# Bias products as units of their own, q and k in quarters, and a newly planned queue in a fused attention and maxout kernel

## The chip, the cores and the metric

The kernel runs on one core of one Trainium2 chip. The metric is the device time of one execution in microseconds (us), the median of several runs. The engines that matter here: PE (TensorE, matrix products), DVE (VectorE), ACT (ScalarE), POOL (GpSimd), and SP (SyncE), which issues nearly all DMAs. Each works through its own queue in program order; semaphores order them among each other.

## The reference

`q`, `k` and `v` have 4 batches, 8 heads, 768 tokens and a head size of 64. The attention is local and global: a token sees the 96 last tokens up to itself and the first 8 tokens of its sequence, with a bias that falls with distance. The result `x` (3072 tokens by 512) goes through a layer that takes the maximum of three products, and one more product.

```python
keep = is_global | is_local              # key position < 8, or 0 <= i - j < 96
scores = scale * q @ k.T - slopes[h] * dist
a = softmax(where(keep, scores, -1e9))
x = (a @ v), heads side by side          # 3072 x 512
h = maximum(maximum(x @ w1, x @ w2), x @ w3)   # 512 -> 768
out = h @ w_out                          # 768 -> 512, float32
```

## The kernel before, in words

The 3072 tokens are 24 tiles T of 128 (6 in each batch). Two tiles make a group G = 0 to 11, which is loaded together. Attention is done tile by tile, against the tile itself and the one before it. The 8 keys of the sequence's start are put into places of the key tile that the local window doesn't reach. The layer that follows is done in chunks c = 0 to 6 of 4, 2, 2, 4, 4, 4 and 4 tiles (`SIZES`), 512 or 256 columns wide, for 6 blocks f of 128 hidden units and 3 weight matrices j.

No scheduler orders the work. The string `SCHEDULE` lists some 770 units; each issues a few instructions, and an engine does what it is given in the order of the list. A unit's name is its code and its arguments, and after `@` the buffer slot that it fills. The waits between engines follow from which buffers the instructions read and write; so the list decides only who stands ahead of whom. The list is the output of a planner outside the kernel.

The units that the text speaks of (line numbers are those of the profile):

- `l` loads q, k (a = 0, 1) or v (a = 2) by DMA on SP (L220). Group number 12 stands for the first four tiles of q or k together, loaded as two halves of four heads (L213). `c` casts them to bf16 (L185), `v` casts v (L238). The last argument of a unit that can run on several engines says which: 0 ACT, 1 DVE, 2 POOL (POOL does a cast in two halves).
- `x` transposes q or k on PE (L252 for the first four tiles, L258 else), `y` copies the result from PSUM (L266, L269). `X` does the same by a DMA transpose.
- `K` and `B` make the tables of masks and biases (L350, L345), after `R`.
- `S T.g.how` makes the scores of a tile for four heads (L321). With `how` = 1 the bias is first put into the same bank by a product with the identity (L313); else `m` multiplies the exponential by a mask on DVE (L337, L339). `e` is the exponential on ACT (L328), from PSUM.
- `A` multiplies the weights with v (L363, L366), `n` divides by the sums on DVE (L374, L375). `t` and `u` transpose the tile on PE and copy it (L390, L393), or `Z` does so by a DMA transpose (L396).
- `G` and `V` put the global keys and values in place (L289 and L291, L299 and L301).
- `w`, `W` and `q`, `Q` load and cast the weights (L488, L185, L497).
- `F c.f.j` is a block of the first layer, 4 products (L405). `f c.f.j` drains it: j = 0 copies the bank (L419, ACT or DVE), j = 1 and 2 take the maximum on DVE (L421, L424).
- `O c.i` is the second layer of one tile, 6 products (L429), `o` copies it from PSUM (L444), `s` stores it (L450), in one DMA or several.
- `E` is the whole second layer of the last chunk, the last tile in pieces of 256, 128 and 128 columns with a copy and a DMA each (L434, L435).
- `D n.w` issues n products of zeros with w columns (L506), fillers on PE.

PSUM has 8 banks. F, O, x and t take one, a pair of scores or an A takes two. A unit that fills a bank waits until the last reader of its former content is through: F waits for an f, S or A for an e or n. The output staging of `o` and `E` uses the buffers of the loaded weights, `wst0` and `wst1`.

Before the first F, PE has the queue's transposes of the first four tiles and of group 2, the scores of tiles 0 to 5, and A and t of tiles 0 to 3, in both queues.

Of the kernel before, what the change touches and what calls it, by code (L numbers as in the profile page):

```python
# [12 lines left out]
FP32 = mybir.dt.float32  # L13
# [36 lines left out]
    V9.1.1 m10.0.1 S10.1.0@0 e10.1@6 V9.0.0 G10.1 O1.1@7 F2.5.1@2 f2.5.1.1 t8@3 F2.4.1@0 O0.0@1 m10.1.1 X11  # L50
    S11.1.0@4 l1.7.2@0 f2.4.0.0@4 o1.1.0@2 e11.1@4 v11.0.0 u8.1@0 S11.0.0@2 v10.0.1 f2.4.1.1 A10@6 V10.0.2
    e11.0@7 V10.1.0 X12@2 o0.0.1@2 n10@0 F2.5.2@0 F2.0.2@1 X13 l2.8.2@0 F2.1.0@4 F2.1.2@5 F2.1.1@2 F2.0.1@3
    m11.1.1 f2.5.2.1@0 Z9 F2.4.2@0 Z10 m11.0.1 f2.1.0.0@1 f2.1.1.1 l2.6.2@1 f2.4.2.1 A11@6 n11@3 O1.0@2
    o1.0.0@1 t11@0 u11.0 F2.3.2@4 l0.7.2@1 f2.1.2.1 f2.0.1.1 f2.0.2.1 f2.3.2.1 F2.2.2@3 l0.8.2@2 v12.0.2
    v12.1.2 v13.1.2 s1.1 f2.2.2.1 v13.0.2 S12.0.0@6 e12.0@1 c0.7.2.2@0 S13.0.0@0 l1.8.2@3 l1.9.2@4 S13.1.0@4
    v16.1.2 S12.1.0@2 l2.7.2@2 F3.0.0@6 G12.1 G13.2 e13.1@2 e13.0@0 e12.1@3 m12.1.1 F3.1.1@7 c1.7.2.2
    F3.0.1@4 m12.0.1 F3.5.0@5 m13.0.1 f3.5.0.1@4 F3.4.0@0 f3.4.0.0@1 f3.0.0.0@3 f3.0.1.1 F3.1.0@1 f3.1.0.0@2
    m13.1.1 F3.1.2@0 F3.5.1@1 v16.0.2 f3.1.1.1 v14.1.2 F3.3.0@6 A13@2 F3.3.2@7 c1.8.2.0@2 F3.5.2@4 V13.1.0
    c1.9.2.0@1 F3.2.1@5 f3.5.1.1 c0.8.2.1 n13@1 V13.0.1 F3.4.1@1 F3.2.0@2 f3.2.0.0@0 f3.1.2.1@1 f3.5.2.1
# [5 lines left out]
    S17.1.0@6 v19.0.0 V15.0.0 e17.1@1 e17.0@3 V15.1.0 O2.0@5 F4.4.0@6 m16.0.1 v19.1.0 s0.1 s3.2 s0.3 s1.0
    o3.0.0@0 m17.1.1 m17.0.1 f4.4.0.1@4 o3.3.1@1 m16.1.1 F4.2.0@7 o3.1.0@0 F4.2.1@0 F4.4.1@1 F4.4.2@4
    f4.4.1.1 F4.3.0@1 A16@2 V16.1.2 f4.2.0.0@0 o2.0.0@1 f4.2.1.1 f4.4.2.1@1 n16@1 X19@1 F4.3.1@0 X18
    S18.1.0@4 f4.3.0.0@2 f4.3.1.1 e18.1@5 S19.1.0@2 V16.0.2 v18.1.2 S19.0.0@6 e19.0@6 m19.0.1 S18.0.0@0
    F4.2.2@4 F4.1.2@5 e18.0@4 l2.10.2@0 m18.1.1 m18.0.1 e19.1@7 A17@0 m19.1.1 F4.5.0@6 f4.5.0.0@1 l1.10.2@6
# [516 lines left out]
```

## Time and profile before

| | |
|---|---|
| median of 3 runs | 176.38 us (176.31 to 176.66) |
| the profiled execution | 176.6 us |
| its span, first to last instruction | 174.7 us |
| PE busy, products | 166.9 us (96%) |
| DVE busy | 127.7 us (73%) |
| ACT busy | 102.4 us (59%) |
| POOL busy | 48.9 us (28%) |
| DMA, moved | 37.35 MB, 214 GB/s in the mean |

The page gives busy times of each engine and the costliest groups of instructions by line. The order of time lists instructions with start and duration, and in brackets how long the engine was idle before and what ended that. The busy time by stretches lists, for each, its length, then the busy time of PE, weight loads, DVE, ACT and POOL with counts, the granted clock, the busy share of the DMA engines and their GB/s. The chain that ended last follows the work back from the last instruction; its rows are start, length and what was run. A busy PE row ends at a modelled end, later than the moment at which the next product may start.

### The profile page before, as it was taken

The numbers are of one execution on the slowest core, as the hardware profiler recorded it, in microseconds if no ns is written. First come the engines' busy times: TensorE is split into PE (matmuls) and PEld (weight loads), VectorE is DVE, ScalarE is ACT, GpSimd is POOL, SyncE is SP. The second block draws the span as 40 slices with busy tenths as digits, with TensorE's granted clock in tenths as the row PEclk, the third lists the DMA queues.
The fourth block names the chain that finished last, engine by engine and source line by source line (L and its number), as shares of the span: only waits on it lengthen the run. The fifth ranks groups of instructions, "written<-read, shape, count | busy, mean of one in ns | idle before, by whom it ended". The sixth has DMA issues, their size and how long they took to land.

```text
span 174.7 us, 3862 instructions
## 1 busy us (share of the span) xinstructions
PE 166.9 (96%) x1489; PEld 93.5 (54%) x1510; DVE 127.7 (73%) x259; ACT 102.4 (59%) x153; POOL 48.9 (28%) x94
## 2 busy tenths in 40 slices
PE   7799999999999999999999999999999999999992
PEld 2346745576956867644456445554444554444442
DVE  7798969784868988589697287839859993059930
ACT  5979895487995876746257994721375651310022
POOL 4056536349370300196614003200203210000000
PEclk9999999999999999999999999999999999999999
DMA  5999999999999898998989498999992134047106
GB/s 148 352 292 312 363 351 379 294 319 345 270 230 267 193 145 194 290 319 198 232 146 196 119 253 200 290 159 260 272 184 68 32 90 64 0 180 240 60 10 234
DMA packets 66658, 37.35 MB, mean 214 GB/s; under 512 B 24144, under 2 KB 61904, under 8 KB 66640
## 3 DMA queue, kind: packets, MB, share of 16 engines
q1 hardware_dynamic: 66496, 37.04, 84.5%
q8 instruction: 12, 0.20, 0.5%
q10 hardware_dynamic: 144, 0.07, 0.1%
q14 instruction: 6, 0.05, 0.1%
HBM read 25.17 MB, written 6.29 MB: 180 GB/s over the span
## 4 chain that ended last, share of the span: by engine, by line
PE 83%; DVE 5%; DMA 4%; ACT 3%; issue 2%; SPq 1%; ACTq 0%
PE psum L405 50%; PE psum L429 18%; PE psum L321 5%; DMA rawqq<-in_q_dram 4%; PE psum L363 4%; PE psum L366 3%; PE psum L258 2%; DVE qkT L266 1%; ACT P L328 1%; PE psum L390 1%; DVE h L421 1%; DVE P L337 1%; PE psum L313 1%; SPq L213 1%; ACT qb L185 1%
## 5 line engine op out<-in xcount | busy, mean ns | idle before, releaser
L405 PE MATMUL psum<-xT,w 128*128 128x512 bf16 (+1 forms) x491 | 99.3, 348 | 1.1
L405 PEld LDWEIGHTS <-w 128*128 128x128 bf16 x504 | 47.5, 98 | 43.1 <-issue 2.7
L328 ACT ACTIVATE P<-psum 128x1024 bf16<-128x1024 f32 (+1 forms) x48 | 43.3, 953 | 13.5 <-PE psum L321 13.2
L421 DVE TENSOR_TENSOR h<-h,psum 128x512 bf16<-128x512 bf16 (+1 forms) x42 | 24.6, 604 | 16.1 <-PE psum L405 12.6
L429 PE MATMUL psum<-wo,ht 128*128 128x512 bf16 (+2 forms) x148 | 32.9, 362 | 0.6 <-issue 0.3
L337 DVE TENSOR_TENSOR P<-P,wmask 128x1024 bf16<-128x1024 bf16 x35 | 23.8, 695 | 6.2 <-ACT P L328 6.1
L424 DVE TENSOR_TENSOR ht<-h,psum 128x512 bf16<-128x512 bf16 (+1 forms) x42 | 26.1, 643 | 3.0 <-PE psum L405 2.4
L419 ACT CAST h<-psum 128x512 bf16<-128x512 f32 (+1 forms) x32 | 15.6, 517 | 20.1 <-PE psum L405 17.9
L429 PEld LDWEIGHTS <-ht 128*128 128x128 bf16 x156 | 14.0, 98 | 14.1
L238 POOL CAST va<-rawv 64x512 bf16<-64x512 f32 x26 | 16.5, 636 | 13.6 <-DMA rawv<-in_v_dram 12.8
L375 DVE TENSOR_TENSOR xb<-psum,rz 128x512 bf16<-128x512 f32 x24 | 16.6, 691 | 0.8
L299 POOL COPY va<-vaf 4x260 int32<-4x260 int32 x15 | 5.9, 395 | 37.5 <-PE psum L366 37.2
L321 PE MATMUL psum<-qkT 64*128 64x128 bf16 x352 | 14.9, 217 | 1.2 <-DVE qkT L266 0.9
L321 PEld LDWEIGHTS <-qkT 64*128 64x128 bf16 x352 | 10.3, 94 | 9.6 <-issue 6.8
L363 PEld LDWEIGHTS <-P 128*128 128x128 bf16 x192 | 12.3, 97 | 2.4
L363 PE MATMUL psum<-va,P 128*128 128x65 bf16 x160 | 12.5, 193 | 0.1
L444 ACT COPY ost<-psum 128x512 f32<-128x512 f32 x11 | 6.4, 589 | 8.9 <-PE psum L429 8.2
L366 PEld LDWEIGHTS <-P 128*128 128x128 bf16 x160 | 10.4, 97 | 1.5 <-issue 0.3
L434 ACT COPY ost<-psum 128x512 f32<-128x512 f32 (+2 forms) x5 | 2.3, 480 | 15.1 <-PE psum L429 15.0
L366 PE MATMUL psum<-va,P 128*128 128x65 bf16 x128 | 9.9, 193 | 0.0
L301 ACT COPY va<-vaf 4x520 bf16<-4x520 bf16 x10 | 6.2, 620 | 3.8 <-PE psum L366 3.7
L374 DVE RECIPROCAL rz<-psum 128x8 f32<-128x8 f32 x24 | 4.8, 202 | 4.7 <-PE psum L366 3.7
(69 smaller groups left out, 134.4 us busy)
## 6 DMA issues: line engine op xcount, KB each, us to landing
rawv<-in_v_dram SPq DMA_DIRECT2D x12, 512.0 KB, 6.3
rawq<-in_q_dram SPq DMA_DIRECT2D x10, 512.0 KB, 7.3
rawk<-in_k_dram SPq DMA_DIRECT2D x10, 512.0 KB, 7.0
out_dram<-ost SPq DMA_DIRECT2D x19, 256.0 KB, 2.6
wst<-in_moe_w_dram SPq DMA_DIRECT2D x3, 1024.0 KB, 10.9
wst<-in_moe_w_dram SPq DMA_DIRECT2D x3, 512.0 KB, 8.1
wost<-in_moe_w_out_dram SPq DMA_DIRECT2D x3, 512.0 KB, 7.3
out_dram<-ost SPq DMA_DIRECT2D x9, 128.0 KB, 1.8
```

What stands on the lines that cost most here:

```text
L238: copies[how](heads(va(T))[64 * e:64 * e + 64, :, 0:D], src)
L321: nc.tensor.matmul(sp[:, hh, j2, ds], qT(T - ds, 1)[hsl, jp], qT(T, 0)[hsl, jp], start=not how, stop=True, skip_group_check=True)
L328: nc.scalar.activation(P[:, :, 0:n], sps[T, g].rearrange("p a b d n -> p (a b) d n")[:, :, 0:n], AF.Exp, bias=0.0, scale=scale)
L337: mul(P, P, wmask[:, g, :, 0:2])
L363: nc.tensor.matmul(o, P[:, i, 0], heads(va(T))[:, h], start=True, stop=(t == 0), skip_group_check=True)
L366: nc.tensor.matmul(o, P[:, i, 1], heads(va(T - 1))[:, h], start=False, stop=True, skip_group_check=True)
L375: nc.vector.tensor_tensor(out=x.rearrange("p (g h) d -> p g h d", g=2), in0=o4[:, :, :, 0:64], in1=rz[:, :, :, None].to_broadcast([128, 2, ...
L405: nc.tensor.matmul(ps, w123[f // 2][:, j, dm, (f % 2) * 128:(f % 2) * 128 + 128], xT[c][:, dm], start=(dm == 0), stop=(dm == 3))
L419: copies[how](h01, ps)
L421: nc.vector.tensor_max(h01s[c, f], h01s[c, f], ps)
L424: nc.vector.tensor_max(dst, h01s[c, f].rearrange("p (t e i) -> p t e i", e=2, i=64), ps.rearrange("p (t e i) -> p t e i", e=2, i=64))
L429: nc.tensor.matmul(po, ht[c][:, f, tt * 128:(tt + 1) * 128], wo[:, f, cols], start=(f == 0), stop=(f == NF - 1))
```

## The change

- **Bias units.** The product that puts the bias into the bank leaves `S` and becomes the unit `b T.g`, which takes the bank's slot. `S` with `how` = 1 adds to it and carries no slot. Seven scores have a bias, as before.
- **Quarters.** The half of q and k that is loaded second (heads 0 to 3 of the first four tiles) is loaded, cast and transposed as two quarters of two heads. `span4` had these parts already; the list used none. A cast on POOL can now be cut along the second dimension too, and the buffer `qkT` of the first two groups is laid out so that each `y` writes one stretch.
- **Staging.** The stores get twelve slots `os` of their own size, laid over the memory of `wst1`, in place of slots of `wst0` and `wst1`.
- **The queue.** The whole list is planned anew, with each buffer held until the instruction that reads it has ended. Units move between engines: DVE takes 15 of the 42 first copies `f` (10 before), 6 of the 20 `o` (9), 2 of the 9 `W` (4), 11 `V` (7), 10 `v` (6); ACT takes 4 of the casts `c` of later groups (9) and 4 `V` (10); POOL 13 such casts (8). One of the two fillers `D3.256` goes. `O5.0` with its copy and its store, now in two DMAs, stands behind `E`.

The diff, cut to its core; of the list, the start, the places named in the text, and the end:

```diff
-    l0.12.1@0 l1.12.1@1 R K4 K3 K6 B4.1 B0.1 K5 K0 K2 B1.0 K7 B6.0 B2.1 l1.12.0@2 B3.1 c0.12.1.1@0 B7.1
-    l0.12.0@3 l2.0.2@0 l2.1.2@1 l0.2.2@4 c1.12.1.1@1 l1.2.2@5 w0.1@0 B5.1 D10.512@0 w0.0@1 x12.0.1@0
-    y0.0.1.0@0 w0.2@2 D3.256@1 x12.1.1@1 y0.1.1.1 S0.1.1@2 c1.12.0.1 c0.12.0.1 S1.1.0@4 K1 x12.1.0@6
-    y0.1.0.1 G0.2 y1.0.1.0@1 e1.1@0 m1.1.1 v0.0.2 v1.0.2 e0.1@1 v0.1.2 D3.256@0 x12.0.0@0 y0.0.0.0 S1.0.1@2
...
-    S6.1.0@4 F0.4.2@2 f0.4.2.1 e7.1@5 F1.5.0@3 F1.1.0@0 m7.1.1 e7.0@6 m7.0.1 F1.3.0@1 F1.5.1@2 x4.1.2@6
...
-    f6.0.1.1 f6.0.2.1 f6.3.2.1 s4.0.2 s4.3.2 s5.2.2 F6.5.0@0 f6.5.0.1@0 F6.5.1@3 f6.5.1.1 F6.5.2@1 f6.5.2.1 E@0
+    l0.12.1@0 l1.12.1@1 D10.512@0 l1.12.3@2 l0.12.2@3 l0.12.3@4 R K7 K6 B1.1 K4 B2.1 K2 B3.0 K1 K5 B0.1 B6.1
+    K0 c0.12.3.2@0 l1.12.2@5 c0.12.1.1 B4.1 B5.1 c1.12.1.1@1 K3 x12.0.1@0 y0.0.1.0@0 B7.1 l2.0.2@0 D3.256@1
+    x12.1.1@1 b0.1@2 v1.0.2 l2.1.2@1 c1.12.3.1 v1.1.2 b1.0@4 y0.1.1.0 b1.1@6 S1.1.1 l0.2.2@6 c0.12.2.1
+    y1.0.1.1@1 y1.1.1.0 x12.0.2@0 e1.1@0 c1.12.2.1 x12.0.3 y0.0.0.1 l1.2.2@0 y1.0.0.1 x12.1.3@1 x12.1.2
...
+    V1.1.1 V1.0.2 G2.1 v3.1.2 w0.2@2 A0@2 S3.0.1 e3.0@6 b3.1@6 n1@0 c0.2.2.2@2 S3.1.1 G3.0 A2@0 V2.0.2
+    e3.1@7 V2.1.2 n0@1 t0@2 W0.0.2 c1.2.2.1 u0.0@0 x2.1.2@3 y2.1.2.0@2 w1.2@2 x2.0.2@2 A3@4 t1@6 u1.0 n2@2
+    y2.0.2.1 t2@7 n3@3 l0.3.2@1 l1.3.2@2 S4.1.0@0 V3.1.2 e4.1@0 V3.0.2 S4.0.0@2 W1.1.2 u2.1 t3@6 G4.1 u3.0
+    W2.0.1 S5.1.0@4 e5.1@2 S5.0.0@0 e5.0@1 m4.1.1 W1.0.1 e4.0@3 F0.5.0@7 F0.4.0@6 W2.1.0 F0.3.0@4 f0.3.0.0@0
...
+    f1.0.1.1 f1.2.0.1@0 Q0.2 f1.0.2.1@1 x3.1.2@6 y3.1.2.1@3 F0.4.2@5 f0.4.2.1 l1.4.2@3 v6.0.2 Q1.2 F1.1.0@0
+    F1.2.2@1 l0.4.2@4 l1.6.2@5 F1.2.1@4 f1.2.1.1 F1.3.1@2 f1.2.2.1 F1.3.2@3 v7.0.2 F1.3.0@4 f1.3.0.0@2
+    f1.3.1.1 f1.3.2.1 x3.0.2@1 F0.5.2@5 f0.5.2.1 F1.4.0@2 F1.1.1@3 f1.1.0.0@3 y3.0.2.0 S6.0.0@0 S6.1.0@4
+    G6.2 c1.4.2.2@1 c0.4.2.2 l0.5.2@0 c0.5.2.2@2 f1.1.1.1 f1.4.0.0@1 e6.0@4 S7.0.0@6 S7.1.0@2 l1.5.2@6
+    c1.5.2.2 e6.1@5 c1.6.2.2@0 e7.1@6 F1.4.1@0 e7.0@7 l2.4.2@1 O0.2@1 f1.4.1.1 m7.1.1 x4.1.2@0 F1.5.2@2
...
+    m10.1.1 e11.0@0 f2.0.0.0@1 A10@2 V10.0.2 f2.1.1.1 m11.1.1 o1.0.0@4 n10@3 Z8@0 V10.1.0 l0.7.2@2 v11.1.2
+    v15.1.2 v12.1.2 F2.5.2@0 O1.1@1 v12.0.2 S12.1.0@2 e12.1@3 S13.1.0@4 m11.0.1 Z9 f2.5.2.1 S13.0.0@6
+    o1.1.1@5 F2.4.2@0 A11@2 n11@2 F2.0.1@1 e13.1@1 F2.3.1@4 m12.0.1 m12.1.1 e13.0@2 c0.7.2.1@1 Z10 f2.0.1.1
...
+    s4.1 f6.1.0.0@1 s3.0 s5.3.2 f6.3.1.1 f6.1.1.1 f6.3.2.1 f6.2.1.1 F6.2.2@2 f6.2.2.1 f6.1.2.1 F6.5.1@4
+    F6.5.0@1 f6.5.0.1@2 F6.5.2@5 f6.5.1.1 f6.5.2.1 E@7 O5.0@2 o5.0.0@5 s5.0.2
...
+    staging = persist.tile([128, 2048 * RINGS["wst1"] + 1024 * RINGS["wst0"]], FP32, name="staging")
+    staged = {"wst1": (0, 2048), "os": (0, 512), "wst0": (2048 * RINGS["wst1"], 1024)}
...
-        n = src.shape[1]
-        for lo, hi in (((0, n // 2), (n // 2, n)) if how == 2 else ((0, n),)):
-            copies[how](dst[:, lo:hi], src[:, lo:hi])
+        if how != 2:
+            copies[how](dst, src)
+            return
+        first = src.shape[1] > 1
+        n = src.shape[1 if first else 2] // 2
+        for half in (slice(0, n), slice(n, 2 * n)):
+            s = (slice(None), half) if first else (slice(None), slice(None), half)
+            copies[how](dst[s], src[s])
...
-            qkT[G] = ring("qkT", slot, [128, 2, 2, NP, 128], BF16, "qkT")
+            shape = [128, 2, 2, 2, NP // 2, 128] if G < 2 and QUAD_USED else [128, 2, 2, NP, 128]
+            qkT[G] = ring("qkT", slot, shape, BF16, "qkT")
...
+    def u_b(slot, T, g):
+        n = 2 if T % NT else 1
+        sp = ring("sp", slot, [128, 2, 2, 2, 128], FP32, "sp")
+        sps[T, g] = sp
+        for hh in range(2):
+            nc.tensor.matmul(sp[:, hh, :, 0:n], identb, bias[:, g, hh, :, 0:2] if n == 2 else bias[:, g, hh, :, 2:3],
+                             start=True, stop=False, skip_group_check=True)
...
     def u_S(slot, T, g, how):
-        if how:
-            for hh in range(2):
-                nc.tensor.matmul(sp[:, hh, :, 0:n], identb,
...
+        if not how:
+            sps[T, g] = ring("sp", slot, [128, 2, 2, 2, 128], FP32, "sp")
+        sp = sps[T, g]
...
-        osts[c, tt] = ring(("wst0", "wst1")[chunks[c][tt] % 2], slot, [128, DM], FP32, "ost")
+        osts[c, tt] = ring("os", slot, [128, DM], FP32, "ost")
```

More of the change, by code (lines that the diff above doesn't have):

```diff
@@ L50 @@
[L50 to L59, printed above, removed]
@@ L65 @@
[L65 to L69, printed above, removed]
@@ L93 @@
-LAST_STAGES = ((2, 1, 0), (2, 0, 1))
+RINGS = {'r': 7, 'rv': 3, 'qb': 3, 'qkT': 4, 'sp': 2, 'h': 8, 'P': 8, 'xb': 4, 'xT': 3, 'wst0': 3, 'wst1': 3, 'ht': 2, 'h01': 5, 'rz': 4, 'os': 12}
+LAST_BANKS = (6, 7, 3, 0, 1, 4, 5, 2)
+LAST_STAGES = (8, 2, 0, 10, 11, 7, 6, 3, 4, 9, 1, 5)
 @with_exitstack
@@ L157, in ring @@
         assert 0 <= slot < RINGS[name]
+        if name in staged:
+            first, width = staged[name]
+            first += slot * width
+            flat = staging[:, first:first + math.prod(shape[1:])]
+            return flat if len(shape) == 2 else flat.rearrange("p (i f) -> p i f", i=shape[1])
         return pools[name].tile(shape, dtype, name=label, tag=f"{name}{slot}")
```

126 lines of the change are left out of this document (66 added, 60 removed).

## The prediction

> **What bounds the kernel now.** I read first the page's totals, then the busy time by stretches, then the chain that ended last.
>
> ```profile
> span 174.7 us, 3862 instructions
> PE 166.9 (96%) x1489; PEld 93.5 (54%) x1510; DVE 127.7 (73%) x259; ACT 102.4 (59%) x153; POOL 48.9 (28%) x94
> PEclk9999999999999999999999999999999999999999
> ```
>
> TensorE is busy 96% of the span and its clock is granted throughout. The busy time by stretches shows where the rest lies:
>
> ```profile
> 24.00:40.00 16.00, 15.89 (x129) 9.44 (x130) 13.74 (x25) 10.49 (x17) 6.91 (x12) 1.00 1.12 331
> 40.00:60.00 20.00, 19.82 (x240) 14.69 (x241) 15.46 (x36) 16.47 (x27) 10.22 (x19) 1.00 1.06 257
> 60.00:80.00 20.00, 19.52 (x190) 12.30 (x193) 15.97 (x34) 13.09 (x21) 6.47 (x11) 1.00 1.03 245
> ...
> sum 144.00, PE 142.23 PEld 79.42 DVE 108.51 ACT 79.79 POOL 38.40; mean PE 20.32 PEld 11.35 DVE 15.50 ACT 11.40 POOL 5.49
> ```
>
> The first number after each stretch's length is PE's busy time. From 24 to 168 us PE is idle for 144.00 - 142.23 = 1.77 us in all. That is nearly everything that a better order can win in the middle (a little more hides behind matmul ends, which are modelled). The new queue has the same 126 F, 24 A, 48 S and 20 O units, and a score run still stands between products of another shape 15 times after the first F in both, so PE's own work there is unchanged. The kernel's time is therefore the **start** (until the first F, L405), the **middle** (PE's work plus its idle) and the **tail** (after PE's last product). The change is judged in these three.
>
> **The start: quarters and bias units.** The chain, the order of time and the groups by shape give the prices:
>
> ```profile
> 17.69 0.89 PE psum L258 x16
> ...
> 19.24 0.24 PE psum L390 x4
> ...
> 21.59 0.32 PE psum L405
> ```
>
> ```profile
> 9.23 1.72 SPq L220 DMA_DIRECT2D rawk<-in_k_dram  x1
> 9.39 0.69 DVE L185 CAST qbq<-rawqq 128x1024 bf16<-128x1024 f32 x1 [0.33 <-DMA rawqq<-in_q_dram]
> ...
> 9.58 0.49 PE L506 MATMUL psum<-zeros 128*128 128x256 bf16 x3
> ...
> 15.40 1.05 ACT L185 CAST qb<-rawq 128x1024 bf16<-128x1024 f32 x1
> ...
> 16.34 1.95 ACT L328 ACTIVATE P<-psum 128x1024 bf16<-128x1024 f32 x2
> ...
> 16.69 0.67 DVE L185 CAST qb<-rawk 128x1024 bf16<-128x1024 f32 x1
> ...
> 18.17 1.01 ACT L269 COPY qkT<-psum 128x1024 bf16<-128x1024 bf16 x1
> ...
> 18.62 0.69 DVE L269 COPY qkT<-psum 128x1024 bf16<-128x1024 bf16 x1
> ```
>
> For the k at 9.23 alone, the time from issue to landing:
>
> ```profile
> DMA to landing us min/median/max: 7.3/7.3/7.3
> ```
>
> ```profile
> L328 ACT ACTIVATE P<-psum 128x1024 bf16<-128x1024 f32 x40 | 39.3, 1022 | 11.9 <-PE psum L321 11.5
> ...
> L328 ACT ACTIVATE P<-psum 128x512 bf16<-128x512 f32 x8 | 4.8, 603 | 1.7 <-PE psum L321 1.7
> ...
> L393 ACT COPY xT<-psum 128x512 bf16<-128x512 bf16 x3 | 1.8, 587 | 1.5 <-PE psum L390 1.5
> ```
>
> ```profile
> L375 DVE TENSOR_TENSOR xb<-psum,rz 128x512 bf16<-128x512 f32 x24 | 16.6, 691 | 0.8
> ...
> L374 DVE RECIPROCAL rz<-psum 128x8 f32<-128x8 f32 x24 | 4.8, 202 | 4.7 <-PE psum L366 3.7 <-PE psum L363 0.7
> ```
>
> The last half of q is cast at 9.39 for 0.69 us now. In quarters the cast that stands last is half as long (about 0.35, an estimate from that row), and so is the block of transposes behind it: some 0.6 us is won there. The three bias units (b0.1, b1.0, b1.1) run before their scores' operands are ready, in PE time that is idle; later, each still costs what it cost inside S. One filler of 0.49 us (9.58) goes; it lay in idle time, so it is worth nothing. Two more issues on SP cost nothing, since SP issues far ahead of the landings there.
>
> But the gain does not reach the first F. k of group 2 (tiles 4 and 5) is issued at 9.23 and lands 7.3 us later, at 16.5, as its cast at 16.69 shows. The same bytes stand ahead of it in the new queue, so it lands at 16.5 again; its cast ends at 17.3 again. The new order then puts both transposes of group 2 (x2.1, x2.0) before A3. x2.0 takes bank 2, which u0.0 empties on ACT after e3.1. The two e3 ran 16.34 to 18.29; with the 1.05 us cast at 15.40 moved to POOL they end about 0.9 earlier, at 17.4. So u0.0 ends at 18.0 (0.59), x2.0 at 18.45 (half of the 0.89 row), A3 near 18.95 (at most the 0.66 that now lies between 18.58 and 19.24). On DVE y2.0.2.1 (0.69, as at 18.62) stands before n3: it starts 0.2 after x2.0, ends at 19.3, and n3 (0.20 + 0.69) at 20.2. t3 is done near 20.6. On ACT stand y2.1 (1.01, to 19.0), u1.0 (behind t1, 19.35 to 19.95), e4.1 (1.02, to 20.95) and then u3.0, to 21.55. The first F starts near 21.6, against 21.59 now: **0**. Bounds: -0.9, if what ACT wins passes through whole, and +0.7, one unit late on POOL, where a cast of 1.05 us on ACT becomes two of about 0.7.
>
> **The middle: the order planned anew.** Nothing computes less. By the groups, DVE takes five more first copies (f with j = 0) and five fewer copies of O and W between them; with the small ones its sum grows by about 2 us, ACT's falls by about 7 and POOL's grows by about 5. The held-buffer rule adds no instruction: the waits were always in the program, only the order is chosen differently.
>
> ```profile
> 41.84 0.24 PE psum L321 x4
> 42.07 0.02 issue
> 42.10 0.61 ACT P L328
> 42.70 0.04 issue
> 42.74 0.38 PE psum L405
> ```
>
> This is the kind of stall that such a rule should remove: the first S of a run writes a bank, its exponential (L328) must read it, and an F of the same bank stands too near. The chain runs through L328 here: it ends at 42.70 and the F starts at 42.74. It costs PE one or two tenths, since other S run meanwhile: all of PE's idle time from 40 to 60 us is 0.18. The old queue has this form three times (S6.0.0 to F0.4.2, S12.0.0 to F3.0.0, S18.1.0 to F4.2.2), the new one once (S6.0.0@0 to F1.4.1@0, with three S between and a half exponential of 0.60: about 0.05). But it has others, where DVE is late:
>
> ```profile
> L337 DVE TENSOR_TENSOR P<-P,wmask 128x1024 bf16<-128x1024 bf16 x35 | 23.8, 695 | 6.2 <-ACT P L328 6.1
> L424 DVE TENSOR_TENSOR ht<-h,psum 128x512 bf16<-128x512 bf16 x30 | 21.0, 724 | 2.6 <-PE psum L405 2.1
> L421 DVE TENSOR_TENSOR h<-h,psum 128x512 bf16<-128x512 bf16 x30 | 19.9, 681 | 15.0 <-PE psum L405 12.6 <-ACT h L419 2.0
> ...
> L424 DVE TENSOR_TENSOR ht<-h,psum 128x256 bf16<-128x256 bf16 x12 | 5.2, 440 | 0.4 <-PE psum L405 0.3
> ```
>
> F1.3.0@4 takes the bank of F1.2.1, whose maximum stands on DVE behind y3.1 (0.69) and f0.4.2 (0.72): about 0.5. S12.1.0@2 takes A10's bank, emptied by n10, which stands behind m11.1 (0.70): 0.2. F2.4.2@0 waits for f2.5.2 (0.44) behind m11.0 (0.70): 0.25. F0.0.1@1 waits for f0.5.1 (0.68): 0.15. With the 0.05 that is about 1.15 us in some 38 us. A part of each stall, the last matmul's modelled end, counts as PE busy, so perhaps 0.6 of it would show as idle. The old kernel shows 0.11 + 0.18 + 0.48 = 0.77 over the 56 us from 24 to 80. So I take the middle at **0**, with ends at -1.8 (all of PE's idle goes) and +1.8 (it doubles).
>
> **The tail: O5.0 after E.** In the old queue E is last, and E ends in small pieces:
>
> ```profile
> 171.63 0.27 ACT L434 COPY ost<-psum 128x128 f32<-128x128 f32 x1 [0.34 <-PE psum L429]
> 171.93 0.37 ACTq L435 DMA_DIRECT2D out_dram<-ost  x1
> ```
>
> ```profile
> L444 ACT COPY ost<-psum 128x512 f32<-128x512 f32 x11 | 6.4, 589 | 8.9 <-PE psum L429 8.2
> ```
>
> Outputs issued on SP in a row, and the time from issue to landing of all outputs after 156 us:
>
> ```profile
> 156.92 3.29 SPq L450 DMA_DIRECT2D out_dram<-ost  x7
> ```
>
> ```profile
> DMA to landing us min/median/max: 1.7/1.9/2.2
> ```
>
> In the new queue `O5.0@2 o5.0.0@5 s5.0.2` follow E. PE ends at the same time, since six products are only moved. But the last copy is 512 wide, 0.59 instead of 0.27: +0.32. Its output goes out in two DMAs on SP, one behind the other: seven issues in 3.29 us are 0.47 each, so the last is issued 0.47 after the first: +0.45 or so. The landing takes 1.7 to 2.2 either way. Nothing runs beside it, PE is done. Tail: **+0.75**; ends +0.3 (the second DMA's issue hides behind the first's landing) and +1.0.
>
> **The sum.** The profiled execution took 176.6 for its span of 174.7; the median of the runs is 176.38, so I take 0.2 off. 176.6 + 0 + 0 + 0.75 - 0.2 = 177.15, say **177.1**.
>
> **The rivals.** (1) *Faster: the bank stalls go.* The new order holds a bank until its reader ends, and the waits of the form at 42.10 go, with the other idle. To show, it must win the tail's 0.75 back and some 0.35 more, out of the 1.77 or at the start. For it: three such stalls become one. Against: the four DVE places. At 1.5 in the middle and 0.4 at the start: 176.4 + 0.75 - 1.9 = 175.2. (2) *No change:* the middle or the start wins just what the tail loses, or the tail's second DMA hides: 176.4. It is also the case in which the change does not do what it says, as the plan's rule has no instruction of its own. (3) *Slower still: DVE becomes the bound* around the change from chunk 0 to 1 and from 2 to 3, and the F behind it wait bank after bank: 177.1 + 1.5 = 178.6. For it: DVE's load grows there while PE's doesn't; against: its 73%. (4) *The PE clock falls* when the filler at 9.58 goes and PE pauses for loads. The products of some 2.5 us between 7 and 12 us would take twice as long, 177.1 + 2.5 = 179.6. The first fillers show the lower rate:
>
> ```profile
> 1.19 4.45 PE L506 MATMUL psum<-zeros 128*128 128x512 bf16 x10 [1.19 <-DVE cap L524]
> ```
>
> Ten of 512 columns in 4.45 us are about 0.44 each. The three of 256 in 0.49 (at 9.58) are at most 0.16 each, and their last end is a modelled one, so the rate by column had risen by then. The Trainium skill, "TensorE: Matmul & The Clock Gate", section "The HAM clock gate", says that the clock halves after an idle window of about 3.4 us. By that rule it would not fall here: the longest pause that I find in the new order is below 1 us. No run here shows such a fall.
>
> **How the numbers follow.** Forecast (177.1, 176.75 to 177.8) 0.42; rival 1: 0.22; rival 2: 0.15; rival 3: 0.18; rival 4: 0.03. About 0.2% (0.35 us) is what a measurement of this kernel can tell from no change. Faster 0.22, same 0.15, slower 0.42 + 0.18 + 0.03 = 0.63. The range reaches from 175.4, near rival 1, to 178.6, rival 3, and leaves out less than 0.2.
>
> **What would show it.** Start: the first L405 product at 21.6 (right) or before 21.0 (wrong). Middle: PE's idle from there to the last F near 1.8 us; below 0.7, rival 1; above 3 with DVE as releaser, rival 3. Tail: the last line in time is L450 on SP twice, 0.47 apart, after a 0.59 us copy, and the span ends 0.75 us later after PE's last product than now. If PE's last product comes over a microsecond earlier, the forecast is wrong.

## The result and the profile after

| | before | after |
|---|---|---|
| median | 176.56 us (176.21 to 177.12, 20 runs) | 176.09 us (175.03 to 177.06, 20 runs) |
| ratio, 95% interval | | 0.997 (0.9958 to 0.9982) |
| the profiled execution, its span | 176.6, 174.7 | 176.69, 174.8 |

The change makes the kernel 0.3% faster, about 0.5 us. The forecast was 177.1, slower. The profiled execution of after lies 0.6 us above its median; a second profile of the same kernel (e1 below, 176.16, span 174.4) lies at it, so both are used.

The totals of the page after, as those shown of before:

```profile
span 174.8 us, 3865 instructions
...
PE 165.9 (95%) x1485; PEld 93.6 (54%) x1507; DVE 131.9 (75%) x268; ACT 95.4 (55%) x147; POOL 54.7 (31%) x99
...
PEclk9999999999999999999999999999999999999998
```

DVE's sum grew by 4.2 us, ACT's fell by 7.0, POOL's grew by 5.8 (forecast: 2, 7 and 5). The clock is granted until the last slice, most of which lies behind PE's last product. The busy time by stretches of after (PE's is the first number behind the length):

```profile
24.00:40.00 16.00, 15.89 (x122) 9.07 (x123) 12.31 (x24) 11.17 (x16) 8.21 (x13) 1.00 1.05 345
40.00:60.00 20.00, 19.83 (x232) 14.85 (x233) 16.11 (x34) 14.00 (x23) 14.49 (x25) 1.00 1.06 235
60.00:80.00 20.00, 19.18 (x211) 12.40 (x212) 17.56 (x41) 11.92 (x19) 4.28 (x9) 1.00 1.10 246
80.00:100.00 20.00, 19.14 (x183) 9.88 (x186) 16.90 (x31) 11.04 (x15) 6.87 (x12) 1.00 0.87 154
...
sum 144.00, PE 141.46 PEld 79.43 DVE 112.01 ACT 73.12 POOL 43.44; mean PE 20.21 PEld 11.35 DVE 16.00 ACT 10.45 POOL 6.21
```

PE's idle time from 24 to 168 us *rose*, from 1.77 to 144.00 - 141.46 = 2.54 us. The rise lies between 60 and 100 us, in two waits:

```profile
PE psum L433 <- DMA xT<-xb: 0.7, 1, 0.7
PE psum L391 <- DVE ht L452: 0.6, 1, 0.6
```

That is the view of who waited for whom (total, times, longest). The first is F3.4.0, which starts at 72.81, after the DMA transpose Z10; the second is A13, which starts at 83.12 and whose banks a maximum (L452) empties late.

By its idle time the middle should have become 0.8 us longer. It became shorter, as the starts of single products show, in profiled executions of these kernels (the e-numbers are the experiments'):

| | first F | first F to last product | last product to span's end | span |
|---|---|---|---|---|
| before | 21.53 | 149.81 | 3.36 | 174.69 |
| after | 21.58 | 149.20 | 4.05 | 174.83 |
| e1, after again | 21.85 | 148.49 | 4.05 | 174.39 |
| e2, O5.0 before E | 21.59 | 148.67 | 3.21 | 173.47 |
| e12, e2 again | 21.63 | 149.12 | 3.21 | 173.96 |
| e5, before with O5.0 behind E | 21.56 | 149.89 | 4.18 | 175.63 |
| e6, e2 with halves | 23.09 | 148.48 | 3.32 | 174.89 |
| e13, before with other banks | 21.38 | 148.81 | 3.40 | 173.59 |

Start and tail came as forecast (0 and +0.7), the middle won 0.6 to 1.3. Of both, 0.16 us is only a matter of where the two are divided: the last product has 512 columns in after, e1 and e5, and 128 in the others, and the difference counts to the tail and not to the middle (0.216 us, worked out below, less 0.89 / 16 = 0.056 for 128 columns, by the prediction's row of L258). So PE's own work and waits won some 0.45 to 1.15.

Where they won is seen in the weight loads better than in the products. The rows of the loads for F, from 22 to 170 us, of before and then of after; the last part is the idle time in front of these loads and what ended it:

```profile
L405 PEld LDWEIGHTS <-w 128*128 128x128 bf16 x501 | 47.3, 98 | 42.9 <-issue 2.7
```

```profile
L433 PEld LDWEIGHTS <-w 128*128 128x128 bf16 x501 | 47.3, 98 | 42.6 <-DMA xT<-xb 0.9 <-issue 0.3
```

The waits of these loads alone, again of before and then of after (total, times, longest):

```profile
PEld L405 <- issue: 2.7, 10, 0.6
```

```profile
PEld L433 <- DMA xT<-xb: 0.9, 1, 0.9
...
PEld L433 <- issue: 0.3, 1, 0.3
```

A load of 0.10 is followed by an idle 0.12 as a rule, since the product behind it takes 0.22; the waits are what goes beyond. In before, loads waited for "issue" 10 times, 2.7 us in all, or about 2.7 - 10 * 0.12 = 1.5 us too long; in after once. One of the ten, in the order of time of before:

```profile
154.82 1.39 PE L405 MATMUL psum<-xT,w 128*128 128x512 bf16 x5
154.88 0.69 DVE L421 TENSOR_TENSOR h<-h,psum 128x512 bf16<-128x512 bf16 x1 [8.63 <-PE psum L405]
155.04 0.31 PEld L405 LDWEIGHTS <-w 128*128 128x128 bf16 x2
...
155.62 0.31 PEld L405 LDWEIGHTS <-w 128*128 128x128 bf16 x2 [0.27 <-issue]
```

F6.1.1 fills bank 6, which F6.2.1 held until the maximum at 154.88 had read it. The maximum ends at 155.57 and the load starts at 155.62, after 0.27 us of idling. The row of the products shows no gap, only 1.39 us for five. Eight products in a row and one alone have these rows in after, the first from the chain, the second from the order of time:

```profile
33.29 1.73 PE psum L433 x8
```

```profile
72.81 0.39 PE L433 MATMUL psum<-xT,w 128*128 128x512 bf16 x1 [0.66 <-DMA xT<-xb]
```

So products start every 1.73 / 8 = 0.216 us, but one alone is drawn as 0.39 long. Five should make 4 * 0.216 + 0.39 = 1.25; the other 0.14 is the wait, and it counts as busy. A stall of up to 0.17 us (0.39 - 0.216) behind each product is invisible as PE idle time.

The start and the tail of after, in the order of time, answer to the rows shown of before:

```profile
16.54 0.73 DVE L195 CAST qb<-rawk 128x1024 bf16<-128x1024 f32 x1
```

```profile
20.95 0.58 ACT L421 COPY xT<-psum 128x512 bf16<-128x512 bf16 x1
```

```profile
171.19 0.58 ACT L471 COPY staging<-psum 128x512 f32<-128x512 f32 x1 [1.03 <-PE psum L457]
171.80 0.81 SPq L477 DMA_DIRECT2D out_dram<-staging  x2
```

The copy u3.0 (L421) ends at 21.53, where 21.55 was worked out, and the first F starts at 21.58.

### The profile page after: what moved, and what is told of

Same layout as the page of the kernel before. It is cut to its first block, busy times and chain, and to the rows that moved or that the text cites. A ratio compares the mean times of both kernels' runs of the same rounds, so it can differ in the third digit from the quotient of the medians.

```text
span 174.8 us, 3865 instructions
## 1 busy us (share of the span) xinstructions
PE 165.9 (95%) x1485; PEld 93.6 (54%) x1507; DVE 131.9 (75%) x268; ACT 95.4 (55%) x147; POOL 54.7 (31%) x99
## 4 chain that ended last, share of the span: by engine, by line
PE 76%; DVE 10%; DMA 6%; ACT 3%; issue 2%; SPq 0%; DVEq 0%
PE psum L433 44%; PE psum L457 17%; PE psum L349 6%; DMA xT<-xb 3%; DMA rawqk<-in_k_dram 3%; DVE P L365 3%; PE psum L391 3%; PE psum L394 2%; PE psum L276 2%; DVE ht L452 1%; DVE xb L403 1%; ACT P L356 1%; PE psum L270 1%; DVE qb L195 1%; PE psum L335 1%
## 5 line engine op out<-in xcount | busy, mean ns | idle before, releaser
L433 PE MATMUL psum<-xT,w 128*128 128x512 bf16 (+1 forms) x491 | 97.5, 348 | 1.5 <-DMA xT<-xb 0.7
L457 PE MATMUL psum<-wo,ht 128*128 128x512 bf16 (+2 forms) x147 | 33.4, 362 | 0.5
L447 ACT CAST h<-psum 128x512 bf16<-128x512 f32 (+1 forms) x27 | 13.8, 523 | 33.1 <-PE psum L433 29.8
L452 DVE TENSOR_TENSOR ht<-h,psum 128x512 bf16<-128x512 bf16 (+1 forms) x42 | 26.2, 644 | 2.1 <-PE psum L433 0.9
L365 DVE TENSOR_TENSOR P<-P,wmask 128x1024 bf16<-128x1024 bf16 x34 | 25.2, 752 | 2.0 <-ACT P L356 1.7
L254 POOL CAST va<-rawv 64x512 bf16<-64x512 f32 x28 | 18.5, 668 | 4.8 <-DMA rawv<-in_v_dram 3.7
L323 POOL COPY va<-vaf 4x260 int32<-4x260 int32 x17 | 7.2, 424 | 34.9 <-PE psum L394 34.5
L201 POOL CAST qb<-rawk 128x512 bf16<-128x512 f32 x12 | 7.5, 654 | 23.7 <-DMA rawk<-in_k_dram 23.7
L447 DVE CAST h<-psum 128x512 bf16<-128x512 f32 (+1 forms) x15 | 9.1, 615 | 5.1 <-PE psum L433 5.1
L471 ACT COPY staging<-psum 128x512 f32<-128x512 f32 x14 | 8.2, 592 | 8.8 <-PE psum L457 8.8
L201 POOL CAST qb<-rawq 128x512 bf16<-128x512 f32 x14 | 8.9, 664 | 9.0 <-DMA rawq<-in_q_dram 5.0
```

The costliest lines, as they stand in the source:

```text
L254: copies[how](heads(va(T))[64 * e:64 * e + 64, :, 0:D], src)
L365: mul(P, P, wmask[:, g, :, 0:2])
L433: nc.tensor.matmul(ps, w123[f // 2][:, j, dm, (f % 2) * 128:(f % 2) * 128 + 128], xT[c][:, dm], start=(dm == 0), stop=(dm == 3))
L447: copies[how](h01, ps)
L452: nc.vector.tensor_max(dst, h01s[c, f].rearrange("p (t e i) -> p t e i", e=2, i=64), ps.rearrange("p (t e i) -> p t e i", e=2, i=64))
L457: nc.tensor.matmul(po, ht[c][:, f, tt * 128:(tt + 1) * 128], wo[:, f, cols], start=(f == 0), stop=(f == NF - 1))
```

## The experiments

The theory: the middle wins by waits for PSUM banks that lie inside PE's busy time, and loses part of it to a few new waits; the tail loses 0.7. Its rivals are named with each run. In the experiments' kernels line numbers are a few lower than in after (F is L429, O and E L453, the maxima L445 and L448, casts L191).

### e1: after, once more

No edit.

> The changed kernel unaltered, as a base on the same chip. Its 20 runs spread from 175.0 to 177.1 us, while those of the kernel before spread from 176.2 to 177.1. If the spread comes from the wait of the first F of chunk 3 (F3.4.0) for a DMA transpose (0.82 us in the first profile), a second profile shows that wait with another length and the span shorter or longer by about as much. If the wait is the same and the time differs, the spread has another cause.

175.92 us (175.05 to 176.54, 12 runs), ratio 0.9967 (0.9949 to 0.9985). The gain is real. F3.4.0 waited 0.37 us in this profile and 0.82 in the first, by the starts of the products on both sides (the view of waits, which counts from a modelled end, has 0.2 and 0.7), so this wait differs from one execution to the next.

### e2, e12, e5: the tail

e2 (and e12, the same kernel in another set of runs) puts O5.0 before E; e5 does the opposite to the kernel before, with one more staging slot:

```diff
-    F6.5.2@5 f6.5.2.1 E@7 O5.0@2 o5.0.0@5 s5.0.2
+    F6.5.2@5 f6.5.2.1 O5.0@2 o5.0.0@5 s5.0.2 E@7
```

```diff
-    O5.0@2 o5.0.0@0 Z23 F6.2.0@3
+    Z23 F6.2.0@3
...
-    s5.0 s5.1
+    s5.1
...
-    F6.5.2@1 f6.5.2.1 E@0
+    F6.5.2@1 f6.5.2.1 E@0 O5.0@1 o5.0.0@3 s5.0.2
```

> O5.0, its copy and its store stand before E again, all else as in the changed kernel. Theory (the tail costs what it lengthens: a copy of 0.58 in place of 0.27, and a second store issued behind the first): 0.6 us less than the changed kernel, about 175.5, with the last product at the same time. Rival (E's own end was waiting for DVE or for the stores, so that O5.0 filled time that was idle anyway): within 0.2 us of the changed kernel, with PE idle in E.

> The kernel after with O5.0, its copy and its store before E, once more, as what the two runs before are compared with. Theory: 174.9 to 175.5, as before; the tail from the last product's start to the span's end 3.2 us. Rival: the earlier 175.04 came from few executions; 175.6 or more.

> The kernel before with O5.0, its copy and its store in two DMAs put behind E (and one more slot of wst0, so that the copy finds a free one). Theory (the tail has a price of its own, whatever the queue in front of it): 0.6 to 0.9 us slower than the kernel before, about 177.3, with the span after the last product starts longer by as much. Rival (the price belongs to the new queue, where E's end meets the stores): within 0.25 of the kernel before.

e2: 175.04 us (174.82 to 175.32), ratio 0.9916 (0.9896 to 0.9935). e12: 175.35, ratio 0.9943 (0.9926 to 0.996). Both beat the kernel before; e2 beats after too, while e12's interval just overlaps that of after (0.9958 to 0.9982). The tail is 3.21 against 4.05 us, 0.84 less. e5: 177.82, ratio 1.007 (1.0049 to 1.0091), 1.2 us slower than before; its tail is 0.82 longer, and its products wait for the DMA transpose Z23 as well, which O5.0 no longer covers:

```profile
PE psum L401 <- DMA xT<-xb: 0.5, 2, 0.3
```

The tail's price is shown from both sides: 0.8 us so measured, or some 0.7 without the 0.16 that is the last product's own. In e2 the loads for F idle 1.1 us less than in before, and its middle is 1.1 us shorter (149.81 - 148.67). That the two agree is in part chance: the runs of score products win some 0.5 us besides (shown below), and e2's waits at O0.1 and A13 (0.5 and 0.4 us) take it back:

```profile
L429 PEld LDWEIGHTS <-w 128*128 128x128 bf16 x501 | 47.4, 98 | 41.8 <-issue 0.3
```

### e9, e13: the kernel before with other banks

e9 gives five products of the last chunk other banks; for that, three copies go to ACT, one of them earlier, and the staging `wst0` gets a fourth slot. e13 is e9 and six more products on other banks. No product changes its place.

```diff
-    o5.1.1@0 o4.3.1@1 s5.3 F6.1.0@7 F6.1.1@6
+    o5.1.0@0 o4.3.0@1 o5.2.0@3 s5.3 F6.1.0@7 F6.1.1@0
...
-    F6.3.0@0
+    F6.3.0@6
...
-    F6.0.0@0 f6.0.0.1@2 o5.2.1@0
+    F6.0.0@4 f6.0.0.1@2
...
-    F6.5.0@0 f6.5.0.1@0 F6.5.1@3 f6.5.1.1 F6.5.2@1
+    F6.5.0@6 f6.5.0.1@0 F6.5.1@3 f6.5.1.1 F6.5.2@4
```

```diff
-    F4.3.0@1
+    F4.3.0@6
...
-    F4.5.1@0 f4.5.1.1 v20.0.1 F5.4.0@3
+    F4.5.1@3 f4.5.1.1 v20.0.1 F5.4.0@0
...
-    F5.2.2@0 f5.4.0.0@0 v23.0.2 F5.5.0@3
+    F5.2.2@3 f5.4.0.0@0 v23.0.2 F5.5.0@0
...
-    F5.3.0@3
+    F5.3.0@0
```

> The kernel before, with other PSUM banks for five products of the last chunk: F6.1.1 takes bank 0 and no longer 6, F6.3.0 bank 6, F6.0.0 bank 4, F6.5.0 bank 6, F6.5.2 bank 4. So that banks 0, 1 and 4 are free by then, the copies o5.1, o4.3 and o5.2 run on ACT and no longer on DVE, o5.2 stands behind o4.3, and a staging slot more is allotted. In the profile of the kernel before, weight loads of L405 wait 0.7 us in 3 places after 145 us, until the copy or maximum of the bank's former content has ended; the product behind each starts later than the one before it allows, by 0.15, 0.08 and 0.13 us, 0.36 in all. Nothing of that is seen as idle time of PE, which is 25.00 - 24.84 = 0.16 us in the whole stretch from 145 to 170. Theory (the new order wins by such waits on banks, which lie inside PE's busy time): the three waits go, and the last product starts 0.3 to 0.4 us earlier; 176.2 to 176.3 against about 176.6. Rival (what counts is PE's visible idle, as the prediction took it): nothing to win here; 176.5 to 176.7.

> The kernel before with the other banks of e9_before_banks and, besides, six more products on other banks: F4.3.0 on bank 6, F4.5.1 on 3, F5.4.0 on 0, F5.2.2 on 3, F5.5.0 and F5.3.0 on 0. In the profile of the kernel before, weight loads of L405 wait behind 104.88 and 118.28 until the copy of the bank's former content has ended; the products behind them are 0.08 us late each. With the 0.36 of the last chunk that makes 0.52 us of hidden waits taken away. Theory (such waits count in full): of the 10 waiting L405 loads of the kernel before at most 5 are left, the last product starts 0.5 us earlier than in the kernel before (149.3 after the first F, against 149.81), and the median is 0.4 to 0.6 us below it. Rival (e9's 0.1 us was all there is, since another engine's chain limits as well): at most 0.2 us below.

e9: 176.29 against 176.4 us, ratio 0.9995 (0.9984 to 1.0006). e13: 175.92 against 176.39, ratio 0.9972 (0.9957 to 0.9987). The loads for F, of e9 and of e13 (L401 here):

```profile
L401 PEld LDWEIGHTS <-w 128*128 128x128 bf16 x501 | 47.3, 98 | 42.5 <-issue 2.1
```

```profile
L401 PEld LDWEIGHTS <-w 128*128 128x128 bf16 x500 | 47.3, 98 | 41.7 <-issue 1.2
```

In e9 the trace did as the theory has it (0.4 us less idle in front of loads, the last product 0.37 earlier), but the time fell by only 0.1, at most 0.28: the rival could not be put aside. e13 did that. It takes away 0.52 us of hidden waits by the count before it ran, and the time fell by 0.47 (0.23 to 0.76), with five waiting loads left, while PE's visible idle in before's last 25 us, where 0.36 of the 0.52 lie, was 0.16 us. That such waits count is shown by this; how much each counts is not. Against e9, on another chip, e13 gains some 0.4 us for six banks that were counted at 0.16, the three copies on ACT have no run of their own, and e13's profiled execution is its fastest (175.45), so that its middle in the table, 1.0 us shorter, is more than the medians show. Still the old order with better banks (and three copies on ACT) gained as much as the whole change did (ratios 0.9972 and 0.997).

### e6: quarters undone; e7: bias units undone

Both on e2. e6 loads, casts and transposes the second half of q and of k in one piece; e7 puts each of the seven bias units directly in front of its score (the second diff shows the first of them).

```diff
-    l1.12.3@2 l0.12.2@3 l0.12.3@4
+    l1.12.0@2 l0.12.0@3
...
-    c0.12.3.2@0 l1.12.2@5 c0.12.1.1
+    c0.12.1.1@0
...
-    c1.12.3.1
+    c1.12.0.1
...
-    c0.12.2.1
...
-    x12.0.2@0 e1.1@0 c1.12.2.1 x12.0.3
+    x12.1.0@1 e1.1@0 c0.12.0.1 x12.0.0@0
...
-    x12.1.3@1 x12.1.2
```

```diff
-    b0.1@2 v1.0.2
+    v1.0.2
...
-    S0.1.1
+    b0.1@2 S0.1.1
```

> As e2 (O5.0 before E), with the second half of q and k of the first four tiles loaded, cast and transposed in one piece each, k first. Theory (the first F waits for group 2's k and what hangs on it, so the quarters are worth nothing): the first F starts within 0.2 us of e2's (21.6) and the time is within 0.3 of e2's 175.0. Rival (the quarters carry the start): the first F starts 0.5 to 0.7 later and the time is 175.6 or more.

> As e2, with each of the seven bias units directly ahead of its score, as inside S before. Theory (the bias products fill idle time at the start at most, and the first F is set elsewhere): first F within 0.2 us of 21.6, time within 0.3 of e2's 175.0. Rival (a bias product in front of its score delays the chain of the first tiles): first F later by 0.5 or more, and the time too.

e6: 176.33 us, ratio 0.9978 (0.9958 to 0.9998), 0.6 to 1.3 us slower than e2 and e12 (by ratios and by medians), and the theory's expectation fell. Two rows of its order of time and one of its chain:

```profile
9.25 0.69 DVE L190 CAST qbq<-rawqq 128x1024 bf16<-128x1024 f32 x1 [0.24 <-DMA rawqq<-in_q_dram]
...
17.98 0.68 DVE L190 CAST qb<-rawk 128x1024 bf16<-128x1024 f32 x1
```

```profile
23.09 0.39 PE psum L428
```

The cast of k of group 2 starts at 17.98 in place of 16.54, and the first F 1.5 us later than in e2. In the new order this cast stands on DVE behind the first tiles' n, and these behind the second half of q. With quarters that chain arrives at 16.54, where the load lands too; with halves it is late. So the quarters are worth 1.5 us at the first F in this order, and the old order reached 21.53 without them. e7: 175.39, ratio 0.9935 (0.9915 to 0.9956), the first F at 21.68: the bias units are worth 0.1 us at the start, and in the time at most some 0.35 (against 175.04 and 175.35), within what these two sets of runs of one kernel differ by.

### e3, e4, e8, e11: the two new waits

e3 and e4 start from after, e8 and e11 from e2. e3 puts Z10 ahead of the load l0.7 and moves the cast of that load back; e4 is e3 with the cast c1.9 on ACT; e8 puts that cast behind n13 on DVE; e11 transposes tile 10 on PE.

```diff
-    l0.7.2@2 v11.1.2
+    v11.1.2
...
-    e13.0@2 c0.7.2.1@1 Z10
+    e13.0@2 Z10 l0.7.2@2
...
-    n12@1
+    n12@1 c0.7.2.1@1
```

```diff
-    c1.9.2.1
+    c1.9.2.0
```

```diff
-    l1.9.2@0 c1.9.2.1
+    l1.9.2@0
...
-    n13@0
+    n13@0 c1.9.2.1
```

```diff
-    F2.0.1@1 e13.1@1
+    F2.0.1@1 t10@7 u10.0 e13.1@1
...
-    c0.7.2.1@1 Z10
+    c0.7.2.1@1
```

> The load l0.7 is issued behind the DMA transpose Z10 rather than before Z8, and its cast c0.7.2.1 stands behind n12; all else as in the changed kernel. Theory (the 0.82 us wait of F3.4.0 is for Z10, which stands in the DMA queue behind that load): the wait goes or falls below 0.2, and the time falls by 0.6 to 0.8, to about 175.4. Rival (DVE is the bound in this stretch, so that the wait only moves to the next bank or to A13): the wait at F3.4.0 goes but the one at A13 grows from 0.54 by as much, and the time stays within 0.3 of 176.1.

> As e3, and the cast c1.9 of 1.1 us moves from DVE to ACT, ahead of the maxima that A13 waits for. Theory (the short waits of the middle are gone in the changed kernel, and two long ones, 0.82 at F3.4.0 and 0.54 at A13, hide most of it): 1.2 to 1.4 us less than the changed kernel, about 174.8. Rival (both waits are one, the DVE's lateness): no more than e3 gives, and the wait turns up at another bank.

> As e2, with the cast c1.9 moved on DVE from in front of the maxima of F3.0 and F3.1 to behind n13. Theory (A13 waits 0.4 to 0.5 us because this cast, 1.1 us long, stands ahead of the maximum that frees A13's bank): the wait at A13 goes, and the time falls by 0.3 to 0.5 to about 174.6. Rival (DVE is late there whatever its order, or X18 then comes late): the wait moves to another bank or to S18 and the time stays within 0.2 of 175.0.

> The kernel after with O5.0 before E, and the transpose of tile 10 on PE (t10, u10) and no longer by DMA (Z10). Theory: the DMA transpose lands late behind loads in part of the executions (F3.4.0 waited 0.82, 0.37 and 1.03 us in three profiles of this order and not at all in two), so its loss is an average of some 0.4 us; PE's transposes cost 0.24 and the copy on ACT 0.59, off the path. No F3.4.0 wait; the median 0.1 to 0.3 us below that of the kernel with O5.0 before E alone. Rival: the median execution has no such wait; 0.2 to 0.3 above.

The theory missed in all four. e3: 177.36, ratio 1.0037 (1.0017 to 1.0057); e4: 177.59, ratio 1.0058 (1.0037 to 1.0078); e8: 175.67, ratio 0.9941 (0.992 to 0.9962); e11: 177.32, ratio 1.0057 (1.0037 to 1.0077). In each the wait aimed at went and another came, which in e8 is what its rival said; of e3, e4, e8 and e11 in turn:

```profile
PE psum L345 <- DMA qkT<-qb: 0.8, 1, 0.8
```

```profile
PE psum L345 <- DMA qkT<-qb: 1.7, 1, 1.7
```

```profile
PE psum L429 <- DVE ht L448: 0.5, 1, 0.5
```

```profile
PE psum L429 <- ACT P L352: 1.6, 1, 1.6
```

In e3 and e4 the load that was moved back makes the scores of tile 14 (L345) late; in e8 DVE is late at F3.4.1 and no longer at A13; in e11 my u10 stands on ACT ahead of e13.1, and the F that takes the score's bank waits for that. The profiled execution of e3 is its fastest (176.2), so its loss of 0.8 us against before, and of 1.4 against after (175.92 in e1), isn't seen in its trace and stays open.

### e10, e14: POOL's casts

Both on e2: e10 moves five casts from POOL to ACT, e14 two from POOL to DVE, behind m6.0.

```diff
-    c0.2.2.2@2
+    c0.2.2.0@2
...
-    c1.5.2.2
+    c1.5.2.0
...
-    c0.6.2.2
+    c0.6.2.0
...
-    c0.11.2.2@1
+    c0.11.2.0@1
...
-    c0.10.2.2@2
+    c0.10.2.0@2
```

```diff
-    c1.5.2.2 e6.1@5 c1.6.2.2@0 e7.1@6
+    e6.1@5 e7.1@6
...
-    m6.1.1 m6.0.1
+    m6.1.1 m6.0.1 c1.5.2.1 c1.6.2.1@0
```

> The kernel after with O5.0 before E, and five casts of later groups (c0.2, c1.5, c0.6, c0.11, c0.10) on ACT and no longer on POOL. Theory: casts on POOL stretch the mask multiplies of DVE that run beside them (0.67 us alone, up to 2.06 in the profile after), and this makes the time differ from one execution to the next; with fewer casts on POOL the longest mask multiply is below 0.9 us, the times of the executions lie within 0.5 us, and the median is 0 to 0.3 us below that of the kernel with O5.0 before E alone. Rival: ACT pays about 5 us more, its exponentials and copies come late, and the median is 0.3 us or more above it, whatever the multiplies do.

> The kernel after with O5.0 before E; the casts c1.5 and c1.6 run on DVE, behind the mask multiply m6.0, and no longer on POOL beside it. In the profile of the kernel with O5.0 before E the two half multiplies m6.1, m6.0 (424 ns each in the median of their form) took 1.56 us at 49.4 while POOL ran four half casts in 2.66 us, and the product O0.1 waited 0.68 us. Theory (POOL's casts stretch DVE's multiplies of two SBUF operands): the two multiplies take 0.85 to 0.9 us, O0.1 waits below 0.1, and DVE's two casts cost what they last only off the path; the median is 0.2 to 0.6 us below that kernel's 175.0 to 175.4. Rival (the multiplies are slow there for another reason): they take 1.5 again and the wait stays, and DVE's 1.4 us more make the time 0.3 us or more longer.

e10: 180.15 us (all six executions), ratio 1.0181 (1.0138 to 1.0224), the slowest of all. Its order of time shows most of it:

```profile
49.74 1.04 ACT L191 CAST qb<-rawk 128x1024 bf16<-128x1024 f32 x1 [3.07 <-DMA rawk<-in_k_dram]
50.69 2.42 ACT L352 ACTIVATE P<-psum 128x512 bf16<-128x512 f32 x3
...
52.25 2.09 PE L429 MATMUL psum<-xT,w 128*128 128x256 bf16 x12 [3.18 <-ACT P L352]
```

The cast c1.5 waits 3.07 us on ACT for its load, the exponentials of tiles 6 and 7 stand behind it, and PE waits 3.18 us for their banks. In e2, with the cast on POOL, PE's longest wait is 0.5 us. The wait has a second price, which the row of the granted clock (tenths, 40 slices) shows:

```profile
PEclk9999999999996999999999999999999999999999
```

From 53 to 56 us, just behind this wait, the granted clock is 0.50, and eight transposes (L272) take 1.04 us at 55.03, where they took 0.61 at 48.45. Of the six executions, the two with a mean clock of 1.0 took 178.32 and 178.62 us, the four with 0.98 to 0.99 took 180.03 to 181.79. So the pause of 3.2 us was followed by a loss of some 1.5 us (an estimate: half of those 3 us); that the other three lost their time in the same way is not shown, since only their mean clock is on record. This is the mechanism of the prediction's rival 4; in after, where PE's longest wait behind the first F is 0.7 us, it does not occur. What the move to POOL is worth here is not the microsecond of ACT but the wait for the load, which no longer stands in front of exponentials.

e14: 175.84, ratio 0.9976 (0.9959 to 0.9994). The same place in e2 and then in e14:

```profile
49.34 2.67 POOL L197 CAST qb<-rawk 128x512 bf16<-128x512 f32 x4
49.40 1.58 DVE L363 TENSOR_TENSOR P<-P,wmask 128x512 bf16<-128x512 bf16 x2
```

```profile
49.59 0.75 DVE L363 TENSOR_TENSOR P<-P,wmask 128x512 bf16<-128x512 bf16 x2
...
50.26 1.29 DVE L191 CAST qb<-rawk 128x1024 bf16<-128x1024 f32 x2
```

```profile
PE psum L453 <- DVE h L445: 0.9, 1, 0.9
```

Two multiplies take 0.75 us without POOL's casts beside them and 1.58 with them: this part of the theory holds. But O0.1 waits longer (0.91 against 0.54 in front of its product), since the two casts now stand on DVE in front of the maximum that it needs. DVE's time there was the matter, whoever takes it: the casts cost it 1.29 us where the stretching had cost 0.83. The time missed too, 0.5 to 0.8 us above e12 and e2 by the medians; more than this one wait explains.

Of the parts of the change, the quarters, the bias units and the tail were undone alone. The staging and most moves of units between engines were not, so the middle's gain is not divided among them.

## Why the prediction was wrong

- **The start, 0:** right, and by the working: the cast of k at 16.54, u3 to 21.53, the first F at 21.58. What was not seen is that the quarters are needed for it (e6).
- **The tail, +0.75:** right. 0.69 between the two profiles, 0.8 in e2 and e5, of which 0.16 is the wider last product. It came by the working: the copy took 0.58 where it took 0.27, and the two issues on SP together 0.81 where one on ACT took 0.37.
- **The middle, 0:** this step failed, and in the step the sentence that PE's idle 1.77 us "is nearly everything that a better order can win". The bracket behind it, "a little more hides behind matmul ends", was where most of the gain lay. In before 1.5 us of waits for banks stood in front of weight loads for F, nearly as large as all visible idle time; the new order took 1.3 of them (ten waiting loads to one). e13 shows that taking such waits away from the old order shortens the time. So the term 0 for the middle should have been some -0.6 to -1.3.
- **The stalls on L328** at 42.10 were taken as the form that the held-buffer rule removes, and were priced at one or two tenths each. They did go, and for more: from the first start in a run of 24 score products to the start of the product behind it took 0.97, 0.98 and 1.13 us in before (from 41.77, 71.68 and 107.49, the three runs that the prediction names) and 1.04, 0.78 and 0.78 in after (from 44.76, 97.82 and 101.55), 0.5 us in all. But the waiting loads for F are mostly another form. Eight of the ten start 0.05 us after another reader's end, a first copy (L419) or a maximum (L421), six of these where a bank was filled again two units of PE later, as in the rows shown. They stood in the order of time of before, as "issue" in front of PEld.
- **The four DVE places** (F1.3.0, S12.1.0, F2.4.2, F0.0.1) show no wait in any profile of the new order. Others do, which I had not named: F3.4.0 for Z10 (0 to 1.03 us, by profile), A13 (0 to 0.6), O0.1 (0.2 to 0.7).
- **The marks** set for rival 1, PE idle below 0.7, would have ruled it out at 2.54, though half of its mechanism is what happened: the bank waits went, the other idle did not. Its price of 175.2, which has the tail's 0.75 in it, was not reached (176.09). The last mark, a last product over a microsecond earlier, was just not reached in e1 (170.34 against 171.33) and further off in after (170.78).
- **Rival 4** rightly did not come. The prediction could say that no run shows a falling clock; e10 now does, behind a wait of 3.2 us.

By the medians: start 0, tail +0.7, so the middle won 1.2 us for the 0.47 measured. e1 has 0.3 - 1.3 + 0.7 = -0.3 in its span.

## What to carry to other kernels

When products queue behind each other on TensorE, read what a better order can win from the idle time in front of the weight loads, less the usual gap, and not from the idle time of the products, whose modelled ends hide stalls of up to 0.17 us each here. An instruction that waits for a load belongs on the engine with the least behind it: one cast that waits for its load made PE wait 3.2 us when it stood on ACT, and the granted clock fell behind that wait. Small work behind the last large piece is paid in full.

## What the hardware showed beside this

DVE's mask multiplies with two operands in SBUF stretch beside POOL's work. All 34 of the full size in after, and the worst place in the order of time:

```profile
L365 DVE TENSOR_TENSOR P<-P,wmask x34: 672/685/2058, 21.1 to 141.5; 128x1024 bf16<-128x1024 bf16 x34
```

```profile
107.98 0.61 POOL L254 CAST va<-rawv 64x512 bf16<-64x512 f32 x1 [0.18 <-DMA rawv<-in_v_dram]
108.19 2.86 DVE L365 TENSOR_TENSOR P<-P,wmask 128x1024 bf16<-128x1024 bf16 x2
108.54 1.16 POOL L201 CAST qb<-rawq 128x512 bf16<-128x512 f32 x2
109.66 0.85 POOL L323 COPY va<-vaf 4x260 int32<-4x260 int32 x1
```

Minimum, median and maximum are 672, 685 and 2058 ns; the two at 108.19 take 2.86 us together while POOL runs four instructions, and POOL's casts keep their usual 0.6. The Trainium skill, "SBUF — State Buffer", section "SBUF: two separate sides", says that DVE and GpSimd share a pair of ports as an exclusive lock, held for a whole instruction, also between a DVE operation with two inputs in SBUF and a GpSimd operation that reads SBUF. The rows agree in kind, and e14, where the casts left, agrees too (1.58 to 0.75 for two halves). They show more than one instruction's hold: the 2058 ns are 1.37 us more than the median, while no POOL instruction there lasts over 0.85 (POOL's spans are rough). Whether this makes the executions of after differ more (175.03 to 177.06) than those of before is open: e14 with fewer such meetings spread as far (175.55 to 177.03).
